# Loads and transposes of the first heads in a routed attention kernel: one load to another queue, one transpose group moved, one dummy product fewer

## The chip, the cores and the metric

The kernel runs on one core of a Trainium2 chip. The metric is the device time of one execution in microseconds, the median of several. Two kernels are compared by runs of the same rounds on the same chip. A profile is of one execution, and times in it count from the start of its span.

## The reference

Four batches of eight heads; 768 positions, head size 64, 16 centroids per head. A query attends to the keys that have the same nearest centroid. A gated feed-forward layer follows.

```python
q_assign = argmax(einsum(q_n, c_n)); k_assign = argmax(einsum(k_n, c_n))
mask = q_assign[..., :, None] == k_assign[..., None, :]
attn = softmax(where(mask, scale * q @ k.T, -1e9)) @ v
x = attn.transpose(0, 2, 1, 3).reshape(B * S, H * D)
xn = x / rms * rms_g                                   # 3072 x 512
out = (silu(xn @ w_gate) * (xn @ w_val)) @ w_out       # d_ff 1536
```

## The kernel before

Before the first scores of head 0 can be computed, its key and query must be loaded, transposed on TensorE (`trans`, tile `tq`, evicted to `qkT`) and multiplied with the transposed centroids (`cblk`). These are the cluster products, tile `sc`. VectorE makes one-hot rows of them, which go below the key and the query (`kext`, `qext`). Dummy products (`busy`, tile `warm`) keep TensorE occupied while the first loads are on their way.

```python
nc.sync.dma_start(out=c_in, in_=centroids...)
load(0, 0)                    # query 0, SyncE's queue
load(0, 1, nc.scalar)         # key 0, ScalarE's queue
load(1, 1, nc.scalar)         # key 1, ScalarE's queue
load(1, 0)
for n in range(2, NQ):        # NQ = 6
    load(n, 1); load(n, 0)
...
busy(WARM)                    # WARM = 7 products of 128 x 512
...
nc.scalar.activation(c_norm, c_ss, ACT.Sqrt)
nc.scalar.activation(first_exp, off, ACT.Exp)     # loads the table early
...
trans(0, 0, 1, nc.vector)     # key 0, evicted by VectorE
centroids_t()                 # c_ps, and two copies to cblk by VectorE
trans(0, 0, 0)                # query 0, evicted by ScalarE
trans(0, 1, 1)                # key 1
pair_clusters(0, (0,))        # cluster products of head 0, VectorE's steps
casts(pool_, 0, K0, Q0, K1)   # GpSimd: bf16 copies into kext, qext
head(0)
trans(0, 1, 0)                # query 1
...
```

Each engine works through its instructions in this order. TensorE may not start the cluster products before the transposes of key 1.

The softmax here doesn't subtract the row's maximum and nothing guards it: scores larger than these inputs give would overflow.

## Time and profile before

| what | value |
|---|---|
| time | 346.06 us (345.69 to 346.11, 3 runs) |
| span of the profile | 344.1 us |
| TensorE on the chain that ended last | 82% of the span |
| key 0, query 0, key 1 land | 3.22, 4.47, 4.66 us |
| cluster products of head 0 start | 6.04 us |

Only the first 7 us are touched. The question is whether those products start earlier, and whether the gain survives to the end. The views, with their lines, are in the prediction below.

### The profile page before, as it was taken

Reading aid. Unit: us, or ns where it says so; the run is one execution under the profiler, and the core shown is the slowest. Engines: PE = TensorE matmul, PEld = TensorE weight load, DVE = VectorE, ACT = ScalarE, POOL = GpSimd, SP = SyncE. Lnnn points to the kernel's source line nnn. Section 1 sums busy time; section 2 is a strip of 40 time slices with the busy share of each in tenths; the row PEclk is TensorE's granted clock in tenths of the full one; section 3 lists DMA queues with packets and bytes.
Section 4 is the critical chain, followed back from the end, with each engine's and each line's share of the span. In section 5 each row is a group of like instructions: output and inputs, shape, how many; then the busy total and the mean of one; then the engine's idle time right before and its main releaser. Section 6 shows DMA issues by size and latency. Waiting matters only on the chain.

```text
span 344.1 us, 8007 instructions
## 1 busy us (share of the span) xinstructions
PE 336.9 (98%) x3045; PEld 208.3 (61%) x3045; DVE 221.7 (64%) x540; ACT 261.1 (76%) x449; POOL 112.7 (33%) x225
## 2 busy tenths in 40 slices
PE   8999999999999999999999999999999999999996
PEld 4547657655766567665665656756566656655654
DVE  6999796984588636795467845686455645575330
ACT  5899979857879878787787878988688887764322
POOL 6999596234335304271131801427000000000000
DMA  8999979873450114401130010000100011001002
GB/s 273 362 226 214 260 161 235 139 248 115 129 177 14 44 56 145 139 17 40 61 94 2 22 57 38 2 3 22 63 32 0 3 41 53 2 1 64 30 2 91
DMA packets 27302, 31.62 MB, mean 92 GB/s; under 512 B 4480, under 2 KB 24320, under 8 KB 27264
## 3 DMA queue, kind: packets, MB, share of 16 engines
q1 hardware_dynamic: 18608, 25.02, 22.3%
q0 software_dynamic: 8368, 5.71, 10.3%
q8 instruction: 24, 0.39, 0.5%
q10 hardware_dynamic: 288, 0.39, 0.4%
q14 instruction: 14, 0.11, 0.1%
HBM read 28.35 MB, written 6.29 MB: 101 GB/s over the span
## 4 chain that ended last, share of the span: by engine, by line
PE 82%; DVE 9%; ACT 6%; issue 2%; DVEq 0%; POOL 0%; ACTq 0%; POOLq 0%
PE o L448 17%; PE gate L423 16%; PE val L423 16%; PE s L333 15%; PE acc L351 9%; ACT pT L337 4%; PE tq L208 3%; PE sc L241 3%; DVE th L432 2%; PE tx L396 1%; DVE gvT L436 1%; ACT th L431 1%; PE warm L117 1%; DVE pads L312 1%; DVE kext L317 1%
## 5 line engine op out<-in xcount | busy, mean ns | idle before, releaser
L337 ACT ACTIVATE pT<-s,off 128x768 bf16<-128x768 f32 x192 | 171.7, 905 | 38.5 <-PE s L333 37.2
L333 PE MATMUL s<-qext,kext 80*128 80x384 bf16 x384 | 94.8, 327 | 1.6 <-ACT pT L337 0.8
L423 PE MATMUL gate<-xnT,wg 128*128 128x384 bf16 x384 | 78.5, 325 | 0.5
L423 PE MATMUL val<-xnT,wv 128*128 128x384 bf16 x384 | 78.1, 325 | 0.2
L432 DVE SCALAR_TENSOR_TENSOR th<-th,gate 128x384 f32<-128x384 f32 x84 | 46.2, 550 | 44.7 <-ACT th L431 43.2
L448 PE MATMUL o<-wo,gvT 128*128 128x512 bf16 x276 | 67.4, 379 | 0.0
L227 POOL CAST qext<-qkT 64x384 bf16<-64x384 f32 x64 | 35.3, 557 | 74.9 <-ACT qkT L214 67.2
L333 PEld LDWEIGHTS <-kext 80*128 80x128 bf16 x384 | 36.3, 98 | 32.7 <-issue 8.1
L436 DVE SCALAR_TENSOR_TENSOR gvT<-th,val 128x384 bf16<-128x384 f32 x84 | 46.4, 552 | 8.1 <-PE val L423 3.6
L423 PEld LDWEIGHTS <-wg 128*128 128x128 bf16 x384 | 36.5, 97 | 24.1 <-issue 2.1
L423 PEld LDWEIGHTS <-wv 128*128 128x128 bf16 x384 | 36.5, 97 | 23.6 <-issue 1.5
L431 ACT ACTIVATE th<-gate 128x384 f32<-128x384 f32 x84 | 41.4, 492 | 10.9 <-PE gate L423 9.9
L351 PEld LDWEIGHTS <-pT 128*128 128x128 bf16 x1152 | 43.4, 97 | 10.1 <-DVE x L358 1.1
L351 PE MATMUL acc<-vbf,pT 128*128 128x65 bf16 x1152 | 45.6, 193 | 0.6 <-ACT pT L337 0.2
L448 PEld LDWEIGHTS <-gvT 128*128 128x128 bf16 x276 | 25.5, 97 | 25.3 <-issue 0.6
L208 PE MATMUL tq<-ident_f,qk 128*128 128x128 f32 x192 | 31.2, 280 | 0.0
L282 POOL DMA_DIRECT2D qext<-oh x40 | 19.1, 487 | 33.6 <-DVE oh L271 33.6
L214 ACT ACTIVATE qkT<-tq 128x384 f32<-128x384 f32 x57 | 26.8, 492 | 2.7 <-PE tq L208 2.2
L397 DVE TENSOR_SCALAR xnT<-tx,gcol 128x384 bf16<-128x384 bf16 x28 | 10.4, 413 | 26.9 <-PE tx L396 26.9
L208 PEld LDWEIGHTS tq<-ident_f,qk 128*128 128x128 f32 x192 | 22.9, 143 | 6.4 <-ACT qkT L214 1.0
L451 ACT COPY o_sb<-o 128x512 f32<-128x512 f32 x23 | 13.5, 586 | 15.2 <-PE o L448 15.2
L282 POOL DMA_DIRECT2D kext<-oh x40 | 19.1, 485 | 8.4 <-DVE inv L356 8.4
(81 smaller groups left out, 247.5 us busy)
## 6 DMA issues: line engine op xcount, KB each, us to landing
qk<-in_q_dram SPq DMA_DIRECT2D x32, 192.0 KB, 3.8
vs<-in_v_dram SPq DMA_DIRECT2D x32, 192.0 KB, 4.2
out_dram<-o_sb SPq DMA_DIRECT2D x23, 256.0 KB, 2.0
qk<-in_k_dram SPq DMA_DIRECT2D x30, 192.0 KB, 4.0
wg<-in_moe_w_gate_dram POOLq DMA_DIRECT2D x4, 384.0 KB, 9.2
wv<-in_moe_w_val_dram POOLq DMA_DIRECT2D x4, 384.0 KB, 11.3
wo<-in_moe_w_out_dram POOLq DMA_DIRECT2D x3, 512.0 KB, 8.3
qext<-oh POOLq DMA_DIRECT2D x40, 12.0 KB, 1.6
```

The source lines that it names most:

```text
L208: nc.tensor.transpose(ps[:, i * P:(i + 1) * P], qk[:, part, 2 * i:2 * i + 2].rearrange("p t d -> p (t d)"), ident_f)
L214: nc.scalar.activation(to, ps, ACT.Copy, scale=by)
L227: on.tensor_copy(to, of)
L282: on.dma_start(out=ext[D:D + NC, h, e * UQ:(e + 1) * UQ], in_=put[g, m][32 * h + e * NC:32 * h + (e + 1) * NC])
L333: nc.tensor.matmul(ps[:, j, :w] if nt == HT else flat[:, j * w:(j + 1) * w], lhsT=cols(kext[g % 4][:KR, hh], g, kc // HT, kc % HT * P, (kc ...
L337: nc.scalar.activation(pT[u, h][:, n * i:n * i + n, :w], of, ACT.Exp, bias=off, scale=scale * ZS)
L351: nc.tensor.matmul(acc[:, h % 2, t], lhsT=pT[u, h][:, kc, t * P:(t + 1) * P], rhs=vbf[g % 4][:, hh, kc % HT * 2 + kc // HT], start=kc == 0 ...
L423: nc.tensor.matmul(ps, lhsT=w[:, c, f * P:(f + 1) * P], rhs=xnT[u][:, c, :n], start=c == 0, stop=c == CC - 1)
L431: nc.scalar.activation(th, ps, ACT.Tanh, scale=0.5)
L432: nc.vector.scalar_tensor_tensor(th, th, 1.0, ps, op0=ALU.add, op1=ALU.mult)
L436: nc.vector.scalar_tensor_tensor(gvT[u][:, f, :n], gates[u], 0.5, ps, op0=ALU.mult, op1=ALU.mult)
L448: nc.tensor.matmul(outs[u], lhsT=gvT[u][:, f, t * P:(t + 1) * P], rhs=wo[:, f], start=f == 0, stop=f == FC - 1)
```

## The change

The intent: key 1 no longer competes with query 0 for the DMA engines, the earlier query is transposed while the centroids' operand is still being made, and with that one dummy product can go.

```diff
-    WARM = 7
+    WARM = 6
@@
     load(0, 0)
     load(0, 1, nc.scalar)
-    load(1, 1, nc.scalar)
+    load(1, 1)
     load(1, 0)
@@
     trans(0, 0, 1, nc.vector)
+    trans(0, 0, 0)
     centroids_t()
-    trans(0, 0, 0)
     trans(0, 1, 1)
```

## The prediction

> **What bounds the kernel now.** I read the page first: busy shares, the slices, the chain that ended last.
>
> ```profile
> span 344.1 us, 8007 instructions
> PE 336.9 (98%) x3045; PEld 208.3 (61%) x3045; DVE 221.7 (64%) x540; ACT 261.1 (76%) x449; POOL 112.7 (33%) x225
> PE   8999999999999999999999999999999999999996
> DMA  8999979873450114401130010000100011001002
> PE 82%; DVE 9%; ACT 6%; issue 2%; DVEq 0%; POOL 0%; ACTq 0%; POOLq 0%
> ```
>
> TensorE is the chain for 82% of the span. DMA is full only in the first slices. The change touches nothing after 7 us, so it can only move the start of the long chain. I therefore read the chain in order of time, and then the timeline of the first 7 us, engine by engine. TensorE (start, duration, engine, line, operation, output<-input, count, and in brackets the idle time before and what ended it):
>
> ```profile
> 3.10 1.06 PE L117 MATMUL warm<-warm 128*128 128x512 bf16 x2
> 3.96 0.84 PE L208 MATMUL tq<-ident_f,qk 128*128 128x128 f32 x3
> 4.60 0.42 PE L182 MATMUL c_ps<-ident_f,c_n 128*128 128x128 f32 x1
> 4.81 0.87 PE L208 MATMUL tq<-ident_f,qk 128*128 128x128 f32 x6
> 6.04 0.84 PE L305 MATMUL sc<-qkT,cblk 128*32 128x384 f32 x4 [0.35 <-DVE cblk L184]
> ```
>
> The dummy products start at 0.99 us, one every 0.427 us, without a gap (the seventh at 3.53), and the transposes of head 0's key follow at 3.96, right behind. Then the centroids, then six transposes (query of head 0, key of head 1), then a wait for VectorE. VectorE in the same stretch:
>
> ```profile
> 4.12 0.25 DVE L178 TENSOR_SCALAR c_n<-c_in,c_inv 128x64 f32<-128x64 f32 x1
> 4.84 0.56 DVE L212 TENSOR_SCALAR qkT<-tq 128x384 f32<-128x384 f32 x1 [0.47 <-PE tq L208]
> 5.31 0.27 DVE L183 COPY cblk<-c_ps 64x128 f32<-64x128 f32 x1
> 5.60 0.29 DVE L184 COPY cblk<-c_ps 64x128 f32<-64x128 f32 x1
> 6.91 0.57 DVE L308 STREAM_TRANSPOSE scT<-sc 64x384 f32<-64x384 f32 x1 [1.02 <-PE sc L305]
> ```
>
> VectorE waits 0.47 us for the key's transposes, then evicts them, copies the centroids' transpose in two halves (each start about 0.29 to 0.47 after the one before), waits 1.02 us for the cluster products, and from 6.91 to about 22 us it has no idle time: the chain in order of time stays on it all that way, then passes to ScalarE's exponentials (about 28 to 38 us), then to TensorE, which from 38.8 us runs practically without a gap. So the quantity to predict is **when the cluster products (6.04 us) start**. ScalarE is the second input of those products (the query's eviction, first half of the pair at 5.39):
>
> ```profile
> 3.74 1.28 ACT L173 ACT_TABLE_LOAD   x1
> 5.03 0.20 ACT L173 ACTIVATE first_exp<-off 128x1 f32<-128x1 f32 x1
> 5.39 0.87 ACT L214 ACTIVATE qkT<-tq 128x384 f32<-128x384 f32 x2 [0.15 <-PE tq L208]
> ```
>
> The loads concerned, from the list of DMA issues (KB each, us from issue to landing): key 0, query 0, key 1 in that order.
>
> ```profile
> qk<-in_k_dram ACTq DMA_DIRECT2D x1, 192.0 KB, 2.5
> ...
> qk<-in_q_dram SPq DMA_DIRECT2D x1, 192.0 KB, 3.3
> ...
> qk<-in_k_dram ACTq DMA_DIRECT2D x1, 192.0 KB, 3.5
> ```
>
> Added to their issues (0.73, 1.18 and about 1.17 us) they land at 3.22, 4.47 and 4.66. The semaphore records give the same, and show that the query's sixteen shares arrive between 3.71 and 4.47, the fifteenth at 4.30. The query of head 1 lands at 5.95: fifteen shares by 5.07, one 0.9 us behind.
>
> **What the Trainium skill says.** "DMA: Bandwidth & Descriptors", section "Issuing engines are not separate DMA queues": DMAs from any issuer run on the same 16 engines, so a second issuer saves only issue time. Section "Queues, rings and completion order": an engine takes turns between the queues that have work. The trace agrees: between about 2.8 and 4.2 us packets of the two queues (1536 B, about 67 ns each on one engine) alternate, so key 1 slows query 0 although they are on different queues. "TensorE: Matmul & The Clock Gate", section "Part 1: The HAM clock gate": the array runs at half clock until about one free-running window of 3.4 us has been busy, with a phase that varies. Here transposes start 0.21 us apart up to 4.81 and 0.11 apart from 4.97 on, so in this execution the clock came at about 4.9 us, 3.9 us after the first dummy. "ScalarE: Activation LUTs", section "What ACT_TABLE_LOAD costs": about 1283 ns; the trace has 1.28 us.
>
> **The change, part by part.**
>
> *One dummy fewer.* Minus one product of 0.427 us: the last of six ends its stream at 3.53. Key 0 has landed (3.22) and its first weight load took 0.23, so it is ready at about 3.5. Transposes of key 0 at 3.53, 3.74, 3.96 (0.21 apart, still half clock), the last over at 3.96 + 0.42 = 4.38. VectorE, free at 4.37, evicts from 4.42: 0.42 earlier than now. TensorE has no gap, so I take the clock's rise at the same 4.9.
>
> *Key 1 behind query 0.* Nothing is added or removed; one issue (0.43 to 0.45 us) moves from ScalarE's queue to SyncE's. ScalarE gains nothing: it waits for the centroids' sum at 3.52 anyway. Query 0 now shares the engines with key 0 alone. When key 0 has landed, query 0 has about half of its eight packets per engine left: 4 x 67 ns = 0.27 us, so an estimated landing of 3.5 to 4.0 instead of 4.47. Key 1 is still complete after 24 packets per engine (key 0, query 0, key 1), hence about 4.6 as now; it is wanted at about 5.0. All later loads on SyncE's queue are issued one issue later, but they wait in a full queue for the engines (4.3 to 4.5 us to landing against 2.5 for the first), so their landings should hardly move.
>
> *Query 0 ahead of the centroids.* The centroids' operand is ready at 4.12 + 0.25 = 4.37, so after a key at 4.17 TensorE would stand 0.2 us; three transposes of the query fill 4.17, 4.38, 4.60 instead. But at half clock they are 3 x 0.21 = 0.64 us, so the centroids' transpose goes at 4.81, where today it goes at 4.60. It starts 0.21 **later**, in spite of the dummy removed. Its end, by today's first query transpose at the same moment (0.33), is 5.14. The copies then start at about 5.17 and 5.46, the products 0.44 after the second copy's start as today (6.04 - 5.60): **5.90**.
>
> *The other input.* The query's transposes are over at 4.60 + 0.42 = 5.02, ScalarE is free at 5.23 after the table load and its small exponential, so it evicts at about 5.26 + 0.49 = 5.75: ready, but only 0.1 us before the other branch. It is a floor: whatever else is won, products before about 5.8 are not possible.
>
> Sum: 6.04 - 5.90 = 0.14 us earlier. Of the 0.43 removed, 0.29 is eaten by the order of the centroids. GpSimd's casts, from 5.46 on also nearly without a gap, win 0.42 on the first and about 0.13 on the second (query eviction 5.88 to 5.75), so they do not hold the chain back. Everything after that is in a fixed order on each engine, so an earlier start should pass through undiminished: 346.06 - 0.14 = 345.9.
>
> **Rivals.**
>
> *The whole dummy counts:* -0.43, 345.6. For it: no idle time between dummies and key. Against it: ScalarE's floor and the centroids behind the query; it needs the full clock about 0.7 us earlier and the query's eviction elsewhere. With an earlier clock alone I get -0.25.
>
> *Query 0 late.* If one slow share makes it land at 4.4 or later, as now, TensorE stands and the centroids come at about 5.0: gain 0 (346.05); with a gap also in the clock's busy window, the full clock may come a window later, and the 0.84 us of cluster products roughly 0.4 us slower: 346.4. Against it: less traffic ahead of it than now.
>
> *Key 1 late.* The products stand behind its transposes in TensorE's order. If it catches the 0.9 us straggler that the third load of SyncE's queue shows now, it lands at 5.5 to 5.9, the products start at 6.1 to 6.3, and the kernel loses up to 0.3: 346.3. I give this one chance in six.
>
> *The gain is given back:* a load that arrives at its fixed time takes up the slack. Head 2's query lands at 6.94 and its transposes are due at about 7.3; value heads land from 10.5 and are cast at 14.7; the gate weights needed near 60 us are in by 50. Little for it; it would make 346.05.
>
> **Range and chances.** Centre 345.9. The rivals span 345.6 to 346.4, and the three runs of before alone spread over 0.42 (345.69 to 346.11). That gives 345.5 to 346.3 for 8 in 10. A change of 2% would be 6.9 us; nothing here is larger than the first 7 us of the kernel, and the movable part is under half a microsecond, so within 2%: 0.98.
>
> **What would show it.** Right: six dummies, key transposes at 3.53; query 0 landing by 4.1; the centroids' transpose at about 4.8; VectorE idle for about 0.25 us between the key's eviction and the centroids' copy; cluster products at about 5.9; the same 0.1 to 0.2 us still there at 22 and at 40 us. Wrong: a gap of TensorE before the query's or key 1's transposes, transposes still 0.21 apart after 5.2 us, or a shift at 7 us that is gone at 40.

## The result, and the profile after

The changed kernel came out at 345.90 us median (345.65 to 346.65, 4 runs), the kernel before at 346.09 (345.69 to 346.17, 4 runs). The ratio is 1.000, 95% interval 0.9983 to 1.0018. (A ratio is the mean time of one kernel's fast runs over that of the other's in the same rounds, so it is not quite the ratio of the medians.) One of the four runs, 346.65, is above all of the kernel before.

The page of the changed kernel's profile, span and the chain by engine:

```profile
span 343.8 us, 8005 instructions
PE 81%; DVE 9%; ACT 6%; issue 1%; DMA 1%; SPq 0%; DVEq 0%; ACTq 0%
```

DMA is new on the chain, with 1%. The chain in order of time says where (start, duration, what):

```profile
1.64 3.64 DMA qk<-in_k_dram
5.29 0.04 issue
5.33 0.55 PE tq L208 x3
5.88 0.79 PE sc L305 x4
```

The chain no longer starts with dummies, the key of head 0 and VectorE. It starts with the load of **key 1**, issued at 1.64 and landed at 5.29, whose transposes stand ahead of the products. TensorE after:

```profile
3.10 0.63 PE L117 MATMUL warm<-warm 128*128 128x512 bf16 x1
3.53 1.12 PE L208 MATMUL tq<-ident_f,qk 128*128 128x128 f32 x6
4.49 0.30 PE L182 MATMUL c_ps<-ident_f,c_n 128*128 128x128 f32 x1
5.33 0.55 PE L208 MATMUL tq<-ident_f,qk 128*128 128x128 f32 x3 [0.55 <-DMA qk<-in_k_dram]
5.81 0.84 PE L305 MATMUL sc<-qkT,cblk 128*32 128x384 f32 x4
```

The last dummy starts at 3.10, the six transposes of key 0 and query 0 follow at 3.53 without a gap, and then TensorE stands for 0.55 us until key 1 has landed. In this execution its full clock comes early: the starts of the transposes go from 0.21 us apart to 0.11 apart at about 4.1. VectorE and ScalarE after:

```profile
4.36 0.56 DVE L212 TENSOR_SCALAR qkT<-tq 128x384 f32<-128x384 f32 x1
4.89 0.28 DVE L183 COPY cblk<-c_ps 64x128 f32<-64x128 f32 x1
5.19 0.29 DVE L184 COPY cblk<-c_ps 64x128 f32<-64x128 f32 x1
6.69 0.58 DVE L308 STREAM_TRANSPOSE scT<-sc 64x384 f32<-64x384 f32 x1 [1.21 <-PE sc L305]
```

```profile
5.06 0.20 ACT L173 ACTIVATE first_exp<-off 128x1 f32<-128x1 f32 x1
5.17 0.47 ACT L214 ACTIVATE qkT<-tq 128x384 f32<-128x384 f32 x1
```

The copies are over at 5.48 and the query's eviction at 5.64. Both inputs of the products wait for TensorE, which is still behind key 1. The loads of query 0 and key 1, from the list of issues (KB, us to landing):

```profile
qk<-in_q_dram SPq DMA_DIRECT2D x1, 192.0 KB, 2.5
...
qk<-in_k_dram SPq DMA_DIRECT2D x1, 192.0 KB, 3.6
```

Query 0 lands 0.76 us earlier than before (3.71 against 4.47), key 1 0.63 later (5.29 against 4.66). The bytes moved show a hole in between: in steps of 0.1 us the rate falls from 369 GB/s at 3.1 us to 77 and 108 at 3.3 and 3.4, and stays at 154 to 261 up to 4.2. In the kernel before it has a shallower dip earlier (169 at the lowest, at 3.1) and is at 415 and 384 at 3.3 and 3.4.

The products start at 5.81 instead of 6.04, 0.23 us earlier. I compared the same TensorE instruction in both traces: at 10, 20 and 40 us and at the end the changed kernel is 0.24, 0.22, 0.23 and 0.24 us ahead. (The one taken for 10 us, here and below, is the first score product `s`, at 10.37 us in the kernel before.) In this pair of profiles the shift at 6 us is thus the shift at the end.

### The profile page after: what moved, and what is told of

The parts are those of the page before. It is cut to its first block, busy times and chain, and to the rows that moved or that the text cites. A ratio compares the mean times of both kernels' runs of the same rounds, so it can differ in the third digit from the quotient of the medians.

```text
span 343.8 us, 8005 instructions
## 1 busy us (share of the span) xinstructions
PE 336.6 (98%) x3044; PEld 208.0 (60%) x3044; DVE 221.4 (64%) x540; ACT 260.9 (76%) x449; POOL 112.8 (33%) x225
## 4 chain that ended last, share of the span: by engine, by line
PE 81%; DVE 9%; ACT 6%; issue 1%; DMA 1%; SPq 0%; DVEq 0%; ACTq 0%
PE o L448 17%; PE gate L423 16%; PE val L423 16%; PE s L333 15%; PE acc L351 9%; ACT pT L337 4%; PE tq L208 3%; PE sc L241 3%; DVE th L432 2%; PE tx L396 1%; DMA qk<-in_k_dram 1%; DVE gvT L436 1%; ACT th L431 1%; DVE pads L312 1%; DVE kext L317 1%
```

## The experiments

Each experiment has one profile, and the instants below are of that one execution. Theory: the cluster products start at the latest of three inputs (the centroids' copies, query 0 on ScalarE, key 1's place on TensorE), and the shift passes to the end. Its rivals: the whole dummy counts; key 1's late landing was chance; the phase of TensorE's clock decides more than the change does. Runs of one call share the runs of the kernel before: 346.16 (345.64 to 346.33, 11 runs) in the first, 346.15 (12 runs, those 11 among them) in the second; the third call was on another chip, with 345.86 (345.62 to 346.55, 9 runs). The diffs of e1, e2, e3, e5 and e7 are against the kernel before, the others against the changed kernel unless said otherwise.

### One dummy fewer alone (e1_warm)

```diff
-    WARM = 7
+    WARM = 6
```

> One dummy fewer alone (loads and order as before). My theory: the start of the cluster products of head 0 is the latest of three inputs (the second copy of the centroids' transpose, the eviction of query 0 on ScalarE, and, by TensorE's order, the transposes of key 1), and what it wins is still there at the end. Here key 0 is transposed from 3.53, the centroids follow at about 4.4 (their operand), query 0 lands at 4.4 to 4.5 and key 1 at 4.6 to 4.8 as before, query eviction at 5.2 to 5.3: products at 5.75 to 5.85 instead of 6.04, and 0.2 to 0.3 us off the end (345.8). Rival 'whole dummy': products at 5.6, 345.65. Rival 'load order is what counts': products at 6.0, 346.05.

Measured: products at 5.88, released by query 0's eviction on ScalarE; shift at the end -0.16.

```profile
5.88 0.84 PE L305 MATMUL sc<-qkT,cblk 128*32 128x384 f32 x4 [0.31 <-ACT qkT L214]
```

Median 345.98 (345.71 to 346.08), ratio 0.9994 (0.9982 to 1.0006). The products were 0.03 us later than expected: the centroids landed 0.17 later than in the profile of before (3.15 against 2.98), and ScalarE's table load started later by the same 0.17 (3.91 against 3.74). The gain is a third of the dummy's 0.43: "the whole dummy" falls, and ScalarE as a limit is seen directly. The full clock came earlier here (between 4.2 and 4.6) than in the profile of before (4.9), so part of the 0.16 may be the clock's.

### Key 1 to the other queue alone (e2_load)

```diff
-    load(1, 1, nc.scalar)
+    load(1, 1)
```

> Key 1 moved to the other queue alone, seven dummies and the old order. My theory: query 0 lands about 0.7 earlier (3.7 to 3.8 instead of 4.47) and key 1 about 0.6 later (5.2 to 5.4 instead of 4.66), because the one queue has no packets ready for a moment at about 3.3 to 3.5. Key 1's transposes then start at about 5.3, the cluster products at 5.9 (as in the changed kernel) or 6.0: at most 0.1 either way, 346.0 to 346.1. Rival 'the late key 1 of the changed kernel was chance (stalled packets)': key 1 lands at 4.6 to 4.8, and no hole in the moved bytes at 3.3 to 3.5.

Query 0 landed at 3.71, and key 1 as in this line, issued at 1.64, at 5.43:

```profile
qk<-in_k_dram SPq DMA_DIRECT2D x1, 192.0 KB, 3.8
```

Products at 6.05, shift at the end -0.02, median 346.08 (345.84 to 346.12), ratio 0.9997 (0.9985 to 1.0009). Both landings are as expected (key 1 0.03 later than the range), so the lateness is not chance. The hole was weak here (338, 323, 261, 261, 230 GB/s from 3.0 to 3.4), so a deep hole is not needed for a late key 1: thirteen of its sixteen shares were in by 4.66, the last came at 5.43. The earlier query buys nothing in the old order, where it is not transposed before 4.81.

### Query 0 ahead of the centroids alone (e3_order)

```diff
     trans(0, 0, 1, nc.vector)
+    trans(0, 0, 0)
     centroids_t()
-    trans(0, 0, 0)
```

> Query 0 ahead of the centroids alone, seven dummies and the old loads. My theory: key 0 is transposed from 3.96, query 0 from about 4.6 (landed at 4.47), the centroids' transpose at about 5.1 instead of 4.60, its copies at 5.3 to 5.4 and 5.6 to 5.7, products at 6.0 to 6.15: nothing won, 0 to 0.1 lost, 346.1. Rival 'the order wins by itself': products before 5.9.

Centroids' transpose at 4.90, products at 6.02, shift at the end -0.04; median 345.85 (345.76 to 346.33), ratio 0.9996 (0.9983 to 1.0009). As expected, nothing is won. The full clock came at about 4.5 here, 0.4 earlier than in the profile of before, and made the order look better than it would at the same clock.

### The changed kernel again (e4_after)

No edit.

> The changed kernel again, to see what of its first 7 us repeats. My theory: query 0 by 3.8, key 1 at 5.1 to 5.4 with the hole in the moved bytes at 3.3 to 3.5, TensorE idle about 0.4 to 0.6 before key 1's transposes, products at 5.75 to 5.95, 345.8 to 345.95. Rival 'chance': key 1 at 4.6 to 4.8 and products at 5.65 to 5.7. The clock's rise may lie anywhere from 4.0 to 5.5.

Five runs at 345.59 to 346.10, and the profiled one at 347.65. In that profile key 1 landed at 5.57, TensorE stood 0.38 us before its transposes, and the transposes were still 0.21 us apart: the full clock came only at about 6.6. Products at 6.44 instead of 5.81; the kernel is 0.49 us behind the kernel before at 10 and 40 us, so the expected 5.75 to 5.95 was missed. The rest of its 1.78 us at the end came in one wait:

```profile
68.63 0.32 PE L333 MATMUL s<-qext,kext 80*128 80x384 bf16 x1 [1.24 <-DMA kext<-oh]
```

That is a small load of one-hot rows, issued at 61.40 us and landed at 68.50. None of the other profiles loses time there. The late key and the gap repeat; the clock's rise, which I had expected between 4.0 and 5.5, came later than that.

### Dummy and order, key 1 on its old queue (e5_warm_order)

```diff
-    WARM = 7
+    WARM = 6
@@
     trans(0, 0, 1, nc.vector)
+    trans(0, 0, 0)
     centroids_t()
-    trans(0, 0, 0)
```

> One dummy fewer and query 0 ahead of the centroids, but key 1 left on the second queue as before. My theory (latest of three inputs; key 1 was late in the changed kernel only because its packets came behind on the one queue): key 1 lands at 4.5 to 4.75, query 0 at 4.3 to 4.5 (later than in the changed kernel), so TensorE may stand up to 0.3 us ahead of the query's transposes; centroids' transpose at 4.9 to 5.1, products at 5.75 to 5.95, 345.85 to 346.0; no wait ahead of key 1. Rival 'it is the dummy alone': the same as the dummy alone, products 5.85 to 5.9. Rival 'the load order is what won': products at 6.0 or later.

A miss. Key 1 landed at 4.42 and query 0 at 4.26, both slightly before the expected ranges, and there was no wait ahead of key 1, but the full clock came at about 6.6: all ten transposes ran at half clock, the centroids' at 5.00, the products at 6.27. Shift at the end +0.36, median 346.30 (346.05 to 346.59, 4 runs), ratio 1.0007 (0.9992 to 1.0021). At half clock the three transposes ahead of the centroids cost 0.64 us, and in this profile the order loses; the ratio is not clear of 1. How the other three runs' clocks stood is not known.

### Products ahead of key 1's transposes (e6_products_first)

```diff
     centroids_t()
-    trans(0, 1, 1)
     pair_clusters(0, (0,))
+    trans(0, 1, 1)
```

> The changed kernel with the cluster products of head 0 ahead of key 1's transposes on TensorE, so that a late key 1 no longer holds them. My theory: products at 5.65 to 5.75, now set by query 0's eviction and the centroids' copies: 0.1 to 0.2 earlier than in the changed kernel, 345.65 to 345.8; key 1's transposes follow the products at about 6.4, and the head after is still in time (VectorE needs its products at about 9.9). Rival 'key 1 was not what held them': products still at 5.8 to 5.9.

The largest miss: median 347.80 (346.40 to 348.10, 6 runs), ratio 1.0037 (1.0021 to 1.0052). In the profile the products started at 6.08, after 0.85 us in which TensorE stood for the centroids' copies, and then ran at half clock for 1.50 us instead of 0.84:

```profile
6.08 1.50 PE L305 MATMUL sc<-qkT,cblk 128*32 128x384 f32 x4 [0.85 <-DVE cblk L184]
```

The clock came at about 10 us. The shift is +1.70 at 10 us and +1.95 at the end. I read this as a gap on TensorE that cost a second window of its clock; one profile suggests it and does not prove it. Whether the order is to blame as well, e11 tells.

### Four dummies more (e7_warm11)

```diff
-    WARM = 7
+    WARM = 11
```

> The kernel before with four dummies more, to measure what a delay at the start costs at the end. My theory (an undiminished shift): the eleventh dummy ends at about 5.2 to 5.3 (the last ones at full clock), products at 6.7 to 6.9 instead of 6.04, and the end later by the same 0.7 to 0.9: 346.8 to 347.0, the shift constant from 10 us to the end. Rival 'given back later': less than half of the shift of the products is left at 40 us and at the end, 346.1 to 346.4.

All eleven dummies ran at half clock, since in this execution the full clock came at about 5.7 though TensorE had been busy without a gap since 0.99. Hence products at 7.47, later than I had written: +1.43. At 10, 20, 40 us and the end the shift is +1.42, +1.41, +1.38, +1.37. Median 347.22 (346.62 to 347.25). A delay of the start is paid in full at the end; "given back later" falls for this path.

### Dummies in the wait for key 1 (e9_fill)

```diff
     centroids_t()
+    busy(2)
     trans(0, 1, 1)
```

> The changed kernel with two dummy products put into the wait for key 1 (behind the centroids' transpose). My theory (a late key 1 lets TensorE stand, and where that idle time falls into the clock's window, the full clock comes 1.5 us or more later): no idle time over 0.3 us between 1.0 and 5.2 us, full clock by 5.0 us, products at 5.75 to 5.95, 345.85 to 346.0, and no run over 346.5. Rival 'the idle time has nothing to do with the late clock': transposes of key 1 at half clock again in some profile, or a run at 346.6 or more. Rival 'the dummies only stand in the way': products at 6.0 or later.

No idle time ahead of key 1, clock at about 5.3, products at 6.08 and not before 5.95: the two dummies, partly at half clock, held key 1's transposes from its landing at 5.09 to 5.59. That is the rival "the dummies only stand in the way", and the clock missed the expected 5.0. Shift at the end 0.00, median 345.98 (345.76 to 346.33, 4 runs), ratio 0.9997 (0.9984 to 1.0010). No run over 346.5, but four runs are too few to call the tail cured.

### Query 0 and key 1 issued one place earlier (e10_cin_act)

```diff
-    nc.sync.dma_start(out=c_in, in_=centroids...)
     load(0, 0)
     load(0, 1, nc.scalar)
+    nc.scalar.dma_start(out=c_in, in_=centroids...)
     load(1, 1)
```

> The changed kernel with the centroids' load moved behind key 0 on the other queue, so that query 0 and key 1 are issued at about 0.74 and 1.18, one issue (0.45 us) earlier each. This is to measure why key 1 lands late, not to win: the centroids land about 0.3 to 0.45 later and hold their own chain. My theory (key 1's packets are not ready when those of query 0 are out, because it is issued third on its queue): key 1 lands at 4.4 to 4.8 instead of 5.1 to 5.6 and the hole in the moved bytes at 3.3 to 3.5 is smaller or gone. Rival 'two rings move more than one, and key 1 on the ring of query 0 is simply slower': key 1 still at 5.1 or later with its issue 0.45 earlier. Products at 5.9 to 6.4 in either case (the centroids' copies), 345.9 to 346.4.

Key 1, issued at 1.17 and still behind query 0 on one queue:

```profile
qk<-in_k_dram SPq DMA_DIRECT2D x1, 192.0 KB, 3.3
```

It landed at 4.45, and the rate between 3.1 and 3.6 us stays at 295 to 376 GB/s, without a hole. An issue 0.47 us earlier brings the landing 0.84 to 1.41 us forward against the three profiles of the changed kernel. So in this one profile key 1 is not late when it is issued second on its queue; sharing the queue with query 0 does not by itself make it late. The place and the time of the issue moved together here, and key 0 landed later too (3.85 against 3.24), so which of these counts is not separated. The centroids landed at 4.63, far later than I had written, and held everything: products at 7.36, median 347.84 (347.19 to 348.67, 4 runs).

### Products first, with dummies in the wait (e11_fill_first)

```diff
     centroids_t()
-    trans(0, 1, 1)
+    busy(2)
     pair_clusters(0, (0,))
+    trans(0, 1, 1)
```

> The changed kernel with the cluster products of head 0 ahead of key 1's transposes, as in the kernel that came out at 347.8, and two dummy products in the wait before them. My theory (that kernel was slow only because TensorE stood for about 0.9 us, so that its clock stayed at half for another window of 3.4 us, up to 10 us): TensorE idle for less than 0.5 us before the products, full clock at or before 7.5 us, products at 5.65 to 6.1 depending on the clock's phase, and a median of 345.6 to 346.0. Rival 'the order itself costs it' (key 1's transposes and all behind them come too late): the median stays above 347.

The products started at 5.64, the earliest of all, and at 10 us the kernel was 0.41 us ahead. At 20 us it was 0.38 **behind**, and so it stayed (+0.40 at the end). Median 346.49 (346.28 to 347.01), ratio 1.0016 (1.0003 to 1.0029). Two lines of its timeline, GpSimd and TensorE, tell where the gain went:

```profile
7.54 0.61 POOL L227 CAST kext<-qkT 64x384 bf16<-64x384 f32 x1 [0.66 <-ACT qkT L214]
...
15.77 0.71 PE L351 MATMUL acc<-vbf,pT 128*128 128x65 bf16 x18 [0.97 <-POOL vbf L230]
```

GpSimd now waits for key 1's eviction (6.99 on ScalarE), its casts follow one another nearly without a gap up to the first value cast at 15.06, and TensorE waits 0.97 us for that cast. In the kernel before, the value cast runs at 14.67 and TensorE has no such wait:

```profile
15.23 0.71 PE L351 MATMUL acc<-vbf,pT 128*128 128x65 bf16 x18
```

So the rival "the order itself costs it" is right in part (the median is not above 347, as it had it): with the clock in order the products come earlier, but a second chain, from key 1 over GpSimd to the values, takes over.

### The changed kernel a third time (e12_after)

No edit.

> The changed kernel a third time, to see whether its slow tail repeats. So far 8 of its 10 runs lie at 345.6 to 346.1 and two at 346.65 and 347.65, while none of the kernel before in 15 runs is over 346.33. My theory (late key 1 leaves a gap in TensorE that in some phases of the clock's window costs half a microsecond or more): key 1 at 5.1 to 5.6 again, median 345.75 to 346.0, and in five or six runs one at 346.4 or more. Rival 'two unlucky runs': all runs within 345.6 to 346.2.

Runs: 348.10 (profiled), 346.26, 346.31, 346.33, 346.40, 345.51; median 346.32, ratio 1.0009 (0.9996 to 1.0023). Key 1 landed at 5.86. TensorE in the profile:

```profile
4.81 0.42 PE L182 MATMUL c_ps<-ident_f,c_n 128*128 128x128 f32 x1
5.91 0.90 PE L208 MATMUL tq<-ident_f,qk 128*128 128x128 f32 x3 [0.68 <-DMA qk<-in_k_dram]
6.74 1.50 PE L305 MATMUL sc<-qkT,cblk 128*32 128x384 f32 x4
```

The products ran at half clock (1.50 us against 0.84). The full clock came at about 9.4, and the kernel was 1.36 us behind the kernel before at 10 us and 2.21 at the end. The median misses the expected 345.75 to 346.0. One run is far out again, but it is the profiled one, as in e4; of those not profiled the slowest is at 346.40, just at the mark I had set. Whether the tail is as heavy without a profile stays open.

### Table load behind query 0's eviction (e13_late_table)

On top of e11:

```diff
-    nc.scalar.activation(first_exp, off, ACT.Exp)   # where the centroids are normed
@@
     trans(0, 0, 0)
+    nc.scalar.activation(first_exp, off, ACT.Exp)
     centroids_t()
```

> As the kernel with the products first and two dummies, and the small exponential that loads ScalarE's table put behind the eviction of query 0, which it delays until 5.2 to 5.3 now. My theory: query 0 is evicted from 4.7 to 5.1, the products are then set by the centroids' copies and the dummies alone: 5.55 to 5.65 in an early phase of the clock, 5.9 to 6.0 in a late one; median 345.5 to 345.9, at best 0.5 below the kernel before. Rival 'the table load only moves': later evictions (query 1, key 2) come 0.5 later and the cluster products of head 1 with them, and the median is no better than 345.85.

Query 0 was evicted at 5.05, not at 4.7, as its transposes ran at half clock; products at 6.08, behind the two dummies. At 10 us the kernel is level with the kernel before (+0.05), at 20 us 0.81 behind, at the end 0.86. Median 346.72 (346.56 to 346.79), ratio 1.0021 (1.0008 to 1.0033). The median is no better, as the rival had it, but its reason is not what this trace shows: key 1's eviction started at 7.44 because TensorE's transposes ended then, and ScalarE had stood 0.38 us for them, after the table load (5.56 to 6.84) and its small exponential. From there the chain goes over GpSimd's casts, as in e11. This profile is useful beside that of e12 for another reason:

```profile
5.02 1.06 PE L117 MATMUL warm<-warm 128*128 128x512 bf16 x2
6.08 0.84 PE L304 MATMUL sc<-qkT,cblk 128*32 128x384 f32 x4
```

Up to 4.81 TensorE's starts are the same to 0.01 us in both profiles. In e12 TensorE then stood for 0.68 us, and its clock rose at 9.4; here dummies ran until the products, and it rose at about 6.0. The rises lie about 3.4 us apart, which is the window that the prediction cites. That both executions had the same phase is assumed and not shown.

## Why the prediction was right or wrong

The number was right, 345.9 against 345.90. It says little about the mechanism, as the forecast gain of 0.14 is smaller than the spread of the runs (0.42 in the three of before). The working was right in its frame and wrong in two steps, which pulled opposite ways in the first profile; that they left products at 5.81, near the predicted 5.90, was luck: in e4 and e12 the same kernel had them at 6.44 and 6.74. One of the prediction's own signs of being wrong, a gap of TensorE before key 1's transposes, showed in all three profiles of the change.

**The frame holds while the products run at full clock and TensorE's transposes behind them are not late.** Then what counts is the start of the cluster products, and a shift there is a shift at the end: -0.23 at 6 us and -0.24 at the end in the changed kernel, -0.16 and -0.16 with the dummy alone, +1.43 and +1.37 with four dummies more. It fails in e11 (-0.40 at the products, +0.40 at the end), e13 (+0.04 and +0.86), e6 (+0.04 and +1.95) and e12 (+0.70 and +2.21). Six dummies and key 0 at 3.53 are as predicted. Query 0 landed at 3.71 to 3.80 in all three profiles, inside the predicted 3.5 to 4.0. ScalarE's floor is real, and in e1 it is the limit, but it lies lower than predicted (query 0's eviction over at 5.64 and not at 5.75): the eviction started at 5.17, before the small exponential was over (5.06 + 0.20), and took 0.47. "Products before about 5.8 are not possible" is therefore wrong: in e11 they started at 5.64.

**Failed step: "Key 1 is still complete after 24 packets per engine (key 0, query 0, key 1), hence about 4.6 as now".** It landed at 5.29, 5.57 and 5.86. The semaphore records show that its sixteen shares split: at 4.66, when the kernel before had all of them, the three profiles had six, eight and seven, all in by 4.33, and the others followed between 4.69 and 5.86. With key 1 issued second, on either queue, all sixteen came within 0.6 us of each other. As I read it, the count of packets holds only while every engine has packets waiting, and behind query 0 some had none of key 1's yet, so that little was moved for some tenths of a microsecond. That is an inference, and why the rate stayed low for longer (up to 4.2 us) and what splits the shares the runs do not tell. In all profiles with key 1 third on the one queue it lands at 5.09 to 5.86 (eight profiles), on ScalarE's queue at 4.40 to 4.66 (five), and one issue earlier on the one queue at 4.45 (e10). I had this as the rival "Key 1 late", with one straggling share as its cause and one chance in six. It happened in every profile of the change, and with eight to ten shares late, not one.

**Failed step: "TensorE has no gap, so I take the clock's rise at the same 4.9".** There is a gap, because key 1 is late, and without one the rise varies too: in the profiles it lies at about 3.9, 4.1, 4.3, 4.4, 4.5, 4.8, 4.9, 5.3, 5.7, 6.0, 6.6 and 6.6, and twice, after gaps of 0.68 and 0.85 us, at 9.4 and about 10. This is the rival "the phase of the clock decides more than the change does", and it stands: with the clock late the copies alone put the products at 6.08 (e6: second copy at 5.64 plus 0.44), and the gain of 0.14 is gone without any late key. In the first profile of the change it was 4.1, so the centroids' transpose, predicted at 4.81 with the clock at 4.9, was at 4.49, and VectorE's predicted wait of 0.25 us did not occur. The early clock moved the limit from the copies (5.90 predicted) to ScalarE: the eviction's end at 5.64 and the step of 0.10 from there to the product (e11: eviction over at 5.54, product at 5.64) give 5.74. The late key took 0.07 of that back, to 5.81. In e4 and e12 the centroids were at 4.81, exactly as worked out, but with key 1 late the products were at 6.44 and 6.74.

**The rival with the second window** was attached to query 0 ("a gap in the clock's busy window"). It came true through key 1, and larger: 0.84 us of products became 1.50 in e12, and the lag at 10 us was 1.36.

**"GpSimd's casts do not hold the chain back"** is right for the first profile of the change. It has little room: once key 1's eviction is near 7 us (e11), they do. The lag of e12 grows between 10 and 20 us (1.36 to 2.32) over GpSimd too, but not through key 1's eviction, at 6.84: its casts stood 1.66 us for the next eviction (9.11 to 9.61), whose transposes had to follow the slow products, and ran nearly without a gap from 9.66; TensorE then stood 0.98 us for the value cast of 17.00 (14.67 in the kernel before).

**What the change is worth.** Over both chips the 16 runs of the changed kernel have a median of 346.04, the 25 timed runs of the kernel before 346.11. Three of the 16 lie above 346.6 (346.65, 347.65, 348.10; the last two are profiled executions), none of the 25. With an early clock it gains about 0.2 us (0.24 in its first profile); a gap with an unlucky phase costs 0.5 us or more (0.49 and 1.36 at 10 us in the other two), and the mean does not move beyond the noise: the three ratios are 1.000, 1.000 and 1.0009. The chips do not even agree on the sign: in the call of e4 its median was 345.84 against 346.16, in that of e12, on the other chip, 346.32 against 345.86, neither clear of noise. No variant was shown to beat both kernels. The dummy alone (345.98, five runs within 345.71 to 346.08, no gap ahead of key 1) is the one I would keep looking at; its gain is inside the noise.

**Open:** what splits the shares of the third load, how often the unlucky phase comes without a profile, and why the small load in e4 was late at 68 us.

## What to carry to other kernels

When a load is moved to another queue, ask not only whom it no longer disturbs but when its own packets will be ready: its place among the issues can cost more than the sharing did. Where dummy products hold TensorE's clock up, a gap behind them can cost more than one of them does (0.49 and 1.36 us at 10 us in e4 and e12, against the 0.16 won with one dummy less), and one profile shows one phase of a clock that differs from run to run. An instruction that is placed ahead of the critical one on an in-order engine puts its own inputs on the critical path, and if it is moved behind, the next consumer of its output may take over.

## What the Trainium skill lacked or had wrong

- "DMA: Bandwidth & Descriptors", section "Issuing engines are not separate DMA queues", says that a second issuer saves only the issue time, which is usually small. Here one place earlier in the issue order of the same queue (0.47 us) moved a landing by 0.84 to 1.41 us (4.45 in e10, one profile, against 5.29 to 5.86). No page says that the rate can fall between two loads that one queue issues 0.46 us apart (77 and 108 GB/s at 3.3 and 3.4 us in the changed kernel, after 369 at 3.1), or that the shares of one load can then land more than a microsecond apart (4.10 to 5.29).
- "TensorE: Matmul & The Clock Gate", section "Part 1: The HAM clock gate", has the window free-running at about 3.4 us, and nothing here contradicts that (e12 and e13 differ by about 3.4), but its "±500ns" for the transition is too narrow here: from 3.9 to 6.6 us in the twelve profiles without a gap over 0.6 us ahead of it, with TensorE started at 0.99 to 1.00 in each; in those without any gap still from 3.9 (e11) to about 6.0 (e13). (Its remark that one kernel showed 6, 11 or 14 slow products allows for more.)
- The same section asks for one busy window but does not say how busy. Here 0.38 us of idle time ahead of the rise left it within the range of the others (e4, clock at 6.6), while 0.68 (e12) and 0.85 (e6) were followed by a rise at 9.4 and about 10: three profiles, so a hint and not a threshold.
- "ScalarE: Activation LUTs", section "What ACT_TABLE_LOAD costs", gives about 1283 ns; the traces have 1.28 us each time, but a drain of the size that the page adds stands neither ahead of the load nor behind it (in the kernel before: activation over at 3.72, load from 3.74 to 5.02, next activation at 5.03).
